# Where the range flag of a fused attention and GELU kernel is combined over partitions, and when the engines load it into registers

## The chip, the cores and the metric

The kernel runs on one core of one Trainium2 chip. The metric is the device time of one launch in microseconds (us), the median of several runs of the same kernel on the same inputs.

## The reference

`q`, `k` and `v` have the shape 8 x 8 x 576 x 64 (batch, head, position, head dimension), float32. Attention runs inside chunks of 64 positions, so every batch and head has nine independent chunks. The attention output, laid out as 4608 tokens of width 512, goes through one feed-forward block with exact GELU.

```python
scores = scale * np.matmul(q_c, k_c.transpose(0, 1, 2, 4, 3))
scores = scores - np.max(scores, axis=-1, keepdims=True)
attn = np.exp(scores)
attn = attn / (np.sum(attn, axis=-1, keepdims=True) + 1e-09)
out = np.matmul(attn, v_c)
...
h = x @ w_in                          # 4608 x 512 by 512 x 2048
g = 0.5 * h * (1.0 + erf(h * inv_sqrt2))
return (g @ w_out).astype(np.float32) # 4608 x 2048 by 2048 x 512
```

## The kernel before

The tokens are worked through in nine tiles of 512 (`NT = B + 1 = 9`): one for the first eight chunks of each batch, and a last one for the ninth chunk of all eight batches. A tile goes through three stages: attention of its chunks, the first product with GELU (`mm1_seven`, helper `seven_rows`), the second product (`mm2_seven`). Both products are done block-wise with seven products instead of eight, so VectorE (DVE in the profile) forms sums of blocks between the matmuls, and ScalarE (ACT) applies exp and GELU and copies out of PSUM. TensorE (PE) is kept busy through nearly the whole kernel; the order of the instructions is written out by hand, in tables of steps per tile, so each engine's queue is fixed.

The fast path leaves out the subtraction of the maximum before the exp. That is sound only as long as no softmax sum gets too small or too large. All reciprocals of the sums are therefore kept in three "homes" of 128 partitions (`early`, `ident_f`, and a part of `rest`), and at the end the kernel asks whether all of them lie between 2^-40 and 2^40. If not, `general()` computes everything again, slowly and safely, in a branch that all five engines take together (`tc.If`, at the end of the program). For the inputs measured here the branch isn't taken.

The question is answered in two steps.

- `range_test` runs on VectorE at slot 6 of the last tile's second product (`e2.setdefault(6, ...)`). Three reductions take the minimum of each home and three the maximum, two comparisons and one more minimum make `good`, one number per partition that is 1 where all is in range.
- `range_count`, after the last tile, multiplies `good` by a column of ones on TensorE, which adds it over the 128 partitions; VectorE copies the count from PSUM to SBUF as an integer (`total`). Then `nc.values_load(total)` loads it into a register of each of the five engines, and the branch compares it with 128.

A register load appears in the trace as TENSOR_LOAD, one for each engine. Five engines means five queues: PE's, DVE's, ACT's, GpSimd's (POOL) and SyncE's (SP). SP issues nearly all stores to DRAM; ScalarE issues some of the last ones.

The last tile's second product ends like this, and here the order around the change is set. Its seven products use three PSUM banks, of which "a" is split in two halves (`m = 0, 1`) of 256 columns. What comes out of them is combined and stored in this order: `done(0, 0)` early (line 726, stores at line 874), then `done(0, 1)` and `done(1, 1)` (line 726 again: one operation on 512 columns, then two on 256), each with its stores at line 874, then `last_piece` twice (line 978: VectorE copies half a bank to `y_sb`; line 981: SP and ScalarE store one half each). TensorE can start the last product on a half of bank "a" only after VectorE has read that half at line 726. After the branch come twelve semaphore waits on SP for all stores and queues, and a barrier of the five engines (all under line 1363, which is the end of the program).

Of the kernel before, what the change touches and what calls it, by code (L numbers as in the profile page):

```python
# [11 lines left out]
def kernel(  # L12
# [9 lines left out]
    nc = tc.nc  # L22
    P = 128
    f32 = mybir.dt.float32
    bf16 = mybir.dt.bfloat16
# [7 lines left out]
    G = H // 2  # L33
# [27 lines left out]
    QD = P // G  # L61
# [17 lines left out]
    NB = MT // 32  # L79
    late = rest[:].bitcast(f32)[:, 256 - 14 * NB:256]  # L80
    homes = [None, ident_f[:], late]
# [26 lines left out]
    work = ctx.enter_context(tc.tile_pool(name="work", bufs=3))  # L108
# [5 lines left out]
    ps_at = ctx.enter_context(tc.tile_pool(name="ps_at", bufs=3, space=bass.MemoryType.PSUM))  # L114
# [452 lines left out]
    def sums_home():  # L567

        raw = stage_tile()[:].rearrange("p (g i n) -> p g i n", g=2, i=4)
        w_in_sum.append([raw[:, 0, i].bitcast(bf16).rearrange("p (k n) -> p k n", k=2) for i in range(4)])  # L570
        kept_more.extend(raw[:, 1, 2 * i:2 * i + 2] for i in range(2))
# [302 lines left out]
            by.dma_start(rows.rearrange("m p d -> p m d"), y_sb[i * CH:(i + 1) * CH])  # L874

    LOW, HIGH = 2.0 ** -40, 2.0 ** 40
    verdict = []

    def range_test():

        assert used == [h.shape[-1] for h in homes]
        n = len(homes)
        for a, op in enumerate((mybir.AluOpType.min, mybir.AluOpType.max)):
            for i, home in enumerate(homes):
                nc.vector.tensor_reduce(ends[:, a, i:i + 1], home, axis=mybir.AxisListType.X, op=op)
        nc.vector.tensor_scalar(ok[:, 0:n], ends[:, 0], LOW, None, op0=mybir.AluOpType.is_gt)
        nc.vector.tensor_scalar(ok[:, n:2 * n], ends[:, 1], HIGH, None, op0=mybir.AluOpType.is_lt)
        nc.vector.tensor_reduce(good, ok, axis=mybir.AxisListType.X, op=mybir.AluOpType.min)
        verdict.append(good)

    def range_count():

        count = ps_at.tile([1, 1], f32, tag="at", name="count")
        nc.tensor.matmul(count[:], ones_1, verdict[0], start=True, stop=True)
        nc.vector.tensor_copy(total, count[:])

    def general():

# [130 lines left out]
    def phase(t, extra2, by_rows=False, first=0, extra1={}, seven=False):  # L1029
        nms = MT // P  # L1030
        order = [(ms, qt) for ms in range(nms) for qt in range(NQ)]
        if by_rows:
            order = [(None, f) for f in range(FF - FC)] + [(ms, NQ - 1) for ms in range(nms)]
        if t not in DENSE:
            mm1_seven(t, extra1)
        else:
            for f in range(first, FF):
                for u in extra1.get(f, ()):
                    u()
                mm1_slot(t, f)  # L1040
        if seven:
            mm2_seven(t, extra2)
            return
        for s, (ms, qt) in enumerate(order):
            for u in extra2.get(s, ()):
                u()
            if ms is None:
                mm2_rows(t, qt)
            else:
                mm2_slot(t, ms, qt)  # L1050
        for u in extra2.get("end", ()):
            u()
# [33 lines left out]
    act_scratch = consts.tile([P, 1], f32, name="act_scratch")  # L1086
    small = consts.tile([P, 28], f32, name="small")
    ends = small[:, 0:6].rearrange("p (a i) -> p a i", a=2)
    ok, good, ones_1 = (small[:, 6:11].bitcast(bf16)[:, a:b] for a, b in ((0, 6), (6, 7), (7, 8)))
    total = small[0:1, 11:12].bitcast(mybir.dt.int32)  # L1090
    nc.gpsimd.memset(ones_1, 1.0)
    homes[0] = consts.tile([P, 3 * NB + 16 + 2 * NB], f32, name="early")[:]

    def act_table(func):
# [2 lines left out]
    with tc.manual_schedule():  # L1097
# [104 lines left out]
        mm, at = (ps_mm, "mm"), (ps_at, "at")  # L1202
# [44 lines left out]
        def flip_qk(t):  # L1247
            for nm in "qk":
                flip(t, nm)
# [6 lines left out]
        for t in range(1, NT):  # L1256
            n = t + 1
            if n < NT:
                tiles[n]["x"] = xpool.tile([P, G, MT], bf16, tag="x", name="x")
            if t == 2:  # L1260
                sums_home()
            if t in STEPS:
                play(t, STEPS[t])
                continue
            if t == 1:
                mm1_slices(1, {0: mm, 1: at, 2: at, 3: mm, 8: mm},
                           (((0, 1, 2), (0,)), last_av, ((0, 1, 2), (1,)), ((3,), (0, 1)), ((8,), (0, 1)),
                            ((0, 1, 2, 3, 8), (2,)), ((0, 3, 8, 1, 2), (3,))))
                x_sums(1)
                for g in range(G):  # L1270
                    cast_qk(2, "k", g, DV)
                flip(2, "q")
                load_v_rows(2, (0,))
                flip(2, "k")
                for ms, y_sb in held:
                    store(0, ms, y_sb)
                held.clear()
                load_v_rows(2, (1,))
                cast_v_rows(2, PO)
                bring_qk(3)  # L1280
            if t > T0 and n + 1 < NT:
                flip_qk(n + 1)
            def next_loads():
                if t + 3 == NT - 1:
                    bring_qk(t + 3)
                elif t + 3 < NT:
                    bring_qk(t + 3)
                if n + 1 < NT:
                    load_v_rows(n + 1)
                    cast_v_rows(n + 1, PO)  # L1290
            if t == T0:
                flip(n + 1, "q")
            elif t > T0:
                next_loads()
            e1, e2 = {}, {}
            exp, gelu = lambda: act_table(Act.Exp), lambda: act_table(Act.Gelu)
            xs = [lambda m=m: quad_x(n, m // 2, m % 2) for m in range(G)]
            g = [[lambda i=i, a=a: g_sum(t, i, a) for i in (1, 2, 4)] for a in range(2)]
            parts = [[lambda m=m: quad_part(t + 2, m // 2, m % 2) for m in ms] for ms in ((1, 0), (3, 2))]
            e1 = {"s3": [lambda: g_sum(t, 3)], "g0": g[0]} if t not in DENSE else {9: [lambda: g_sum(t, 3)], 13: g[0]}  # L1300
            e2 = {0: g[1][:2], 2: g[1][2:]}
            if t <= T0:
                ov = [lambda m=m: quad_over(n, m) for m in range(G)]
                rx = [[lambda m=m: att_rc(n, m), lambda m=m: quad_x_plain(n, m)] for m in range(G)]
                e2 = {0: [exp, lambda: quad_scores(n, ALONE)] + g[1][:2], 2: g[1][2:],
                      4: [lambda: [quad_sums(n), quad_turned(n)]], 5: [ov[0]], 6: [ov[1]],
                      7: [ov[2]] + rx[0], 8: [ov[3]] + rx[1], 9: rx[2], 10: rx[3]}
                e2[{1: 7, 2: 5, T0: 6}[t]].insert(1, lambda: quad_av(n, ALONE))
                if t > 1:
                    e1["x"] = [lambda: x_sums(t)]  # L1310
                if t == T0:
                    e1["g0"] = g[0][:1] + [lambda: w_in_sums(3, (0, 1))] + g[0][1:] + [lambda: w_in_sums(3, (2, 3))]
                if t == 1:
                    e1["w"] = [lambda: weight_sum(2), lambda: weight_sum(3)]
                    e1["w0"] = [lambda: w_in_sums(0, (0, 1))]
                    e1["w1"] = [lambda: w_in_sums(0, (2, 3))]
                    e2[2].append(lambda: weight_sum(4))
                    e2[4].append(lambda: load_qk(4, "q"))
                    e2[7].append(lambda: pool_cast_qk(4, "q"))
                    e2[12] = [lambda: flip_qk(3), lambda: load_qk(4, "k"), lambda: pool_cast_qk(4, "k"),  # L1320
                              lambda: load_v_rows(3), lambda: cast_v_rows(3, PO)]
                else:
                    e1["k"] = [lambda: flip_qk(n + 1) if t < T0 else flip(n + 1, "k"), next_loads]
                if t < T0:
                    e2[11] = [gelu]
                else:
                    e2[2] += [lambda: g_sum(t, 3)]
                    e2[10] += [lambda: quad_scores(n + 1, BETWEEN), gelu]
                    e2[12] = [lambda: x_sums(n)] + parts[0]
                    e2[13] = parts[1]  # L1330
            if t in WHOLE:
                e1, e2 = whole_hooks(t)
            if t == NT - 1:
                e2.setdefault(6, []).append(range_test)
            phase(t, e2, first=5 if t == 1 else 0, extra1=e1, seven=True)
        range_count()
        in_range = nc.values_load(total)
        with tc.If(in_range < P, preferred_fallthrough_block=False):
            general()
# [1 line left out]
_INS = ['q', 'k', 'v', 'moe_w_in', 'moe_w_out']  # L1341
# [26 lines left out]
```

## Time and profile before

| | us |
|---|---|
| median of 3 runs | 266.9 |
| lowest and highest of them | 266.48, 267.42 |
| the profiled execution's own time | 267.09 |
| span of the profiled execution | 265.5 |
| PE busy in the span | 256.1 (96%) |
| DVE busy | 223.1 (84%) |
| ACT busy | 190.5 (72%) |
| POOL busy | 103.2 (39%) |

The span runs from the first to the last instruction in the profile; 267.09 - 265.5 = 1.6 us of the profiled execution lie outside it. Instructions of the sequencers (branches, semaphore waits, register loads, the issuing of DMAs) aren't counted as busy; in the trace their engine's name carries a q (SPq, ACTq).

### The profile page before, as it was taken

What the parts mean: (1) busy time and instruction counts of PE and PEld (TensorE: products, weight loads), DVE (VectorE), ACT (ScalarE), POOL (GpSimd) and SP (SyncE); (2) the same over time, 40 slices, a digit from 0 to 9 for tenths busy, and PEclk for the clock granted to TensorE, in tenths of its full rate; (3) what the DMA queues carried; (4) which work ended last, traced back from release to release, by engine and by line L of the source; (5) the groups of instructions that cost most, each with busy time, mean ns of one, the idle gap of its engine ahead of it and who ended that gap; (6) DMA issues with size and microseconds to landing.
All of it is one profiled execution on the core that took longest, in us unless ns stands there. A gap on an engine that the chain in (4) does not pass through costs nothing.

```text
span 265.5 us, 7854 instructions
## 1 busy us (share of the span) xinstructions
PE 256.1 (96%) x3122; PEld 210.6 (79%) x3122; DVE 223.1 (84%) x394; ACT 190.5 (72%) x386; POOL 103.2 (39%) x225
## 2 busy tenths in 40 slices
PE   6789999999999999999999999999999999999993
PEld 2478875556888888887888888888888888888882
DVE  6874986898897599678999999999999999948772
ACT  3856758987767987898888588947894789227720
POOL 7767778702364291481372095009411300000000
PEclk9999999999999999999999999999999999999998
DMA  6999998999979979999999988998973410130014
GB/s 201 268 311 396 395 401 236 283 193 289 243 195 284 220 175 244 275 239 249 276 245 232 267 186 237 217 175 195 264 160 80 134 42 2 41 119 3 2 40 125
DMA packets 123416, 54.02 MB, mean 203 GB/s; under 512 B 97776, under 2 KB 120304, under 8 KB 123376
## 3 DMA queue, kind: packets, MB, share of 16 engines
q1 hardware_dynamic: 123072, 53.23, 77.4%
q8 instruction: 25, 0.41, 0.7%
q10 hardware_dynamic: 304, 0.26, 0.3%
q14 instruction: 15, 0.12, 0.1%
HBM read 36.70 MB, written 9.44 MB: 174 GB/s over the span
## 4 chain that ended last, share of the span: by engine, by line
PE 76%; DMA 10%; ACT 7%; SPq 4%; issue 1%; DVE 0%; POOL 0%
PE hs_ps L601 31%; PE y_ps L761 22%; PE y_ps L791 13%; DMA arrival<-in_moe_w_out_dram 8%; ACT h L609 3%; SPq L181 2%; PE h_ps L491 2%; DMA arrival<-in_moe_w_in_dram 2%; PE av_ps L349 2%; PE h_ps L481 2%; ACT pT L272 2%; SPq L142 1%; PE y_ps L1025 1%; PE y_ps L989 1%; PE s_ps L264 1%; ACT L1095 1%
## 5 line engine op out<-in xcount | busy, mean ns | idle before, releaser
L609 ACT ACTIVATE h<-hs_ps 128x512 bf16<-128x512 f32 x87 | 49.6, 609 | 6.5 <-PE hs_ps L601 5.7
L238 POOL CAST v_nat<-arrival 128x256 bf16<-128x256 f32 x56 | 24.9, 473 | 33.5 <-DMA arrival<-in_v_dram 23.1
L601 PEld LDWEIGHTS <-w_in_sb 128*128 128x128 bf16 x348 | 33.9, 98 | 4.7 <-issue 0.2
L194 POOL CAST q_nat<-arrival 128x256 bf16<-128x256 f32 x40 | 16.8, 467 | 50.2 <-DMA arrival<-in_k_dram 25.3
L601 PE MATMUL hs_ps<-x,w_in_sb 128*128 128x256 bf16 x232 | 31.8, 272 | 0.0
L761 PEld LDWEIGHTS <-h 128*128 128x128 bf16 x240 | 23.2, 98 | 2.8
L1095 ACT ACT_TABLE_LOAD x16 | 20.5, 1283 | 1.3 <-PEq L1352 1.0
L190 POOL CAST k_nat<-arrival 128x256 bf16<-128x256 f32 (+1 forms) x44 | 19.1, 476 | 5.3 <-DMA arrival<-in_k_dram 5.3
L721 ACT COPY kept<-y_ps 128x512 f32<-128x512 f32 (+1 forms) x17 | 9.0, 536 | 16.0 <-PE y_ps L761 15.9
L761 PE MATMUL y_ps<-w_out_sb,h 128*128 128x256 bf16 x160 | 18.6, 273 | 0.0
L761 PE MATMUL y_ps<-v_bd,k_bd 128*128 128x256 bf16 x160 | 18.5, 273 | 0.1
L761 PEld LDWEIGHTS <-k_bd 128*128 128x128 bf16 x160 | 15.6, 98 | 2.1 <-issue 0.2
L618 ACT COPY hs_ps<-hs_ps 128x512 f32<-128x512 f32 x29 | 16.2, 583 | 0.6 <-PE hs_ps L601 0.5
L601 PE MATMUL hs_ps<-k_bd,w_in_sb 128*128 128x256 bf16 x116 | 16.6, 272 | 0.0
L493 ACT ACTIVATE h<-h_ps 128x512 bf16<-128x512 f32 x21 | 12.5, 604 | 5.5 <-PE h_ps L465 4.1
L272 ACT ACTIVATE pT<-s_ps 128x512 bf16<-128x512 f32 x28 | 14.4, 599 | 1.8 <-PE s_ps L264 1.8
L791 PEld LDWEIGHTS <-h 128*128 128x128 bf16 x144 | 13.8, 98 | 1.7
L465 PE MATMUL h_ps<-x,w_in_sb 128*128 128x256 bf16 x128 | 14.5, 273 | 0.1
L601 PE MATMUL hs_ps<-k_bd,w_in_more 128*128 128x256 bf16 x96 | 14.2, 273 | 0.0
L601 PEld LDWEIGHTS <-w_in_more 128*128 128x128 bf16 x128 | 12.5, 98 | 2.0 <-issue 0.3
L726 DVE TENSOR_TENSOR kept<-y_ps,kept 128x512 f32<-128x512 f32 (+1 forms) x16 | 10.4, 651 | 4.3 <-PE y_ps L761 2.3
L465 PEld LDWEIGHTS <-w_in_sb 128*128 128x128 bf16 x128 | 12.3, 98 | 2.1 <-DVE w_in_sb L1070 0.7
(175 smaller groups left out, 638.9 us busy)
## 6 DMA issues: line engine op xcount, KB each, us to landing
arrival<-in_v_dram SPq DMA_DIRECT2D x58, 128.0 KB, 3.2
arrival<-in_k_dram SPq DMA_DIRECT2D x28, 256.0 KB, 5.6
arrival<-in_q_dram SPq DMA_DIRECT2D x7, 1024.0 KB, 6.9
out_dram<-kept SPq DMA_DIRECT2D x24, 256.0 KB, 3.2
arrival<-in_moe_w_out_dram SPq DMA_DIRECT2D x4, 1024.0 KB, 12.1
arrival<-in_moe_w_in_dram SPq DMA_DIRECT2D x6, 512.0 KB, 8.5
out_dram<-y_sb SPq DMA_DIRECT2D x8, 256.0 KB, 2.5
arrival<-in_v_dram SPq DMA_DIRECT2D x28, 64.0 KB, 2.7
```

What stands on the lines that cost most here:

```text
L190: copy(st[nm][:, q0:q0 + n, g], st[nm + "f"][:, 2 * q0:2 * (q0 + n), g].rearrange("p (q r) d -> p q r d", r=2))
L194: copy(st[nm][:, g, j:j + 2].rearrange("p j r d -> p r j d"), st[nm + "f"][:, 2 * g:2 * g + 2, j:j + 2])
L238: copy(st["v"][:, r::2, n], st["vf"][:, r::2, n])
L272: nc.scalar.activation(pT[:].rearrange("p u (c j) -> p u c j", j=J), tiles[t]["s_ps"][m // 2][m % 2][:].rearrange("p u (j c) -> p u c j", ...
L465: nc.tensor.matmul(to[:, cols], left, right[:, cols], start=(start and a == 0), stop=stop, skip_group_check=True)
L493: nc.scalar.activation(tiles[t]["h"][:, f, :], h_ps[:], Act.Gelu)
L601: nc.tensor.matmul(hs[:, f], left[:, ks, f * P:(f + 1) * P], right[:, ks], start=(fresh and f == 0 and ks == 0), stop=(ks == 1), skip_grou ...
L609: nc.scalar.activation(h[:, n:n + HM, HD * c:HD * (c + 1)], src, Act.Gelu)
L618: "s11": lambda: AC(place_of("b")[:], bank["a"][:]),
L761: nc.tensor.matmul(to, left(f, m), right[:, f], start=(fresh and (split or m == 0) and f == 0), stop=(f == HF - 1), skip_group_check=True)
L791: nc.tensor.matmul(bank[name][:, m], left(f, m), right[:, f], start=(fresh and m == 0 and f == 0), stop=(f == HF - 1), skip_group_check=True)
L1095: nc.scalar.activation(act_scratch[:], rest[:, 0:1], func)
```

## The change

The combination over partitions moves from TensorE to VectorE and into `range_test`, right behind `good`. A 32 x 32 block transpose of `good`, spread over 32 columns, puts the 32 numbers of each of the four partition groups into rows; a reduction takes the minimum of each row; three operations on single numbers take the minimum of the groups at partitions 0, 32, 64 and 96; a comparison turns it into `bad`, an integer that is 1 when anything was out of range. The matmul, its copy, and GpSimd's memset of the column of ones go. `ok` and `good` are float32 instead of bfloat16.

The five register loads are split. SP and GpSimd load `bad` at the end of `range_test`, that is at slot 6 of the last tile; ScalarE at slot 10 of it; TensorE and VectorE where all five stood before, after the last tile. The branch tests the register itself.

```diff
     LOW, HIGH = 2.0 ** -40, 2.0 ** 40
-    verdict = []
...
-        n = len(homes)
+        MIN, n = mybir.AluOpType.min, len(homes)
...
-        nc.vector.tensor_reduce(good, ok, axis=mybir.AxisListType.X, op=mybir.AluOpType.min)
-        verdict.append(good)
-
-    def range_count():
-
-        count = ps_at.tile([1, 1], f32, tag="at", name="count")
-        nc.tensor.matmul(count[:], ones_1, verdict[0], start=True, stop=True)
-        nc.vector.tensor_copy(total, count[:])
+        nc.vector.tensor_reduce(good, ok, axis=mybir.AxisListType.X, op=MIN)
+        turned = work.tile([P, NB, 32], f32, tag="rc", name="turned", bufs=4)[:, 0]
+        nc.vector.transpose(turned, good.to_broadcast([P, 32]))
+        nc.vector.tensor_reduce(good, turned, axis=mybir.AxisListType.X, op=MIN)
+        for s in range(1, G):
+            nc.vector.tensor_tensor(good[0:1], good[0:1], good[QD * s:QD * s + 1], op=MIN)
+        nc.vector.tensor_scalar(bad, good[0:1], 0.5, None, op0=mybir.AluOpType.is_lt)
+        read_flag((mybir.EngineType.SP, mybir.EngineType.Pool))
+
+    flag = nc.alloc_registers("flag")
+
+    def read_flag(engines):
+        for reg in flag:
+            if reg.engine in engines:
+                nc.reg_load(reg, bad)
...
-    ok, good, ones_1 = (small[:, 6:11].bitcast(bf16)[:, a:b] for a, b in ((0, 6), (6, 7), (7, 8)))
-    total = small[0:1, 11:12].bitcast(mybir.dt.int32)
-    nc.gpsimd.memset(ones_1, 1.0)
+    ok, good = small[:, 6:12], small[:, 12:13]
+    bad = small[0:1, 13:14].bitcast(mybir.dt.int32)
...
             if t == NT - 1:
                 e2.setdefault(6, []).append(range_test)
+                e2.setdefault(10, []).append(lambda: read_flag((mybir.EngineType.Activation,)))
             phase(t, e2, first=5 if t == 1 else 0, extra1=e1, seven=True)
-        range_count()
-        in_range = nc.values_load(total)
-        with tc.If(in_range < P, preferred_fallthrough_block=False):
+        read_flag((mybir.EngineType.PE, mybir.EngineType.DVE))
+        with tc.If(flag, preferred_fallthrough_block=False):
             general()
```

Three queues change near the end. SP's, before: the stores of whole blocks (line 867), five stores of line 874, two of line 981, then the register load and the branch.

```order
L867 DMA out_dram<-kept 128x2x256 x3
L867 DMA out_dram<-y_sb 128x2x256
L874 DMA out_dram<-kept 64x2x256 x5
L981 DMA out_dram<-y_sb 64x256 x2
L1337 TENSOR_LOAD small
L1338 COMPARE_AND_BRANCH
L1338 UNCONDITIONAL_BRANCH
```

And SP's queue after the change, from the same place on (the later lines have moved by five or six numbers):

```order
L867 DMA out_dram<-kept 128x2x256 x3
L867 DMA out_dram<-y_sb 128x2x256
L874 DMA out_dram<-kept 64x2x256 x2
L901 TENSOR_LOAD small
L874 DMA out_dram<-kept 64x2x256 x3
L987 DMA out_dram<-y_sb 64x256 x2
L1343 COMPARE_AND_BRANCH
L1343 UNCONDITIONAL_BRANCH
```

The load has moved ahead of the last five stores of SP, and nothing but the branch stands behind them now. On ScalarE it moves in the same way, ahead of its three stores, and on GpSimd it stays last.

VectorE's queue before, from the last step of `range_test` to the branch:

```order
L888 TENSOR_REDUCE small<-small 128x1
L726 TENSOR_TENSOR kept<-y_ps,kept 128x512
L726 TENSOR_TENSOR kept<-y_ps,kept 128x256 x2
L978 COPY y_sb<-y_ps 128x256 x2
L895 COPY small<-count 1x1
L1337 TENSOR_LOAD small
L1338 COMPARE_AND_BRANCH
```

The same stretch of VectorE's queue after the change (line 887 is the former 888, line 984 the former 978):

```order
L887 TENSOR_REDUCE small<-small 128x1
L889 STREAM_TRANSPOSE turned<-small 128x32
L890 TENSOR_REDUCE small<-turned 128x1
L892 TENSOR_TENSOR small<-small 1x1 x3
L893 TENSOR_SCALAR small<-small 1x1
L726 TENSOR_TENSOR kept<-y_ps,kept 128x512
L726 TENSOR_TENSOR kept<-y_ps,kept 128x256 x2
L984 COPY y_sb<-y_ps 128x256 x2
L901 TENSOR_LOAD small
L1343 COMPARE_AND_BRANCH
```

Six operations have come in ahead of line 726, and the copy of the count behind line 978 has gone. Everything earlier in the program stands in the same order on every engine, apart from GpSimd's one memset at the start.

## The prediction

> **What bounds the kernel now.** I began with the page: its span, the busy times and the chain that ended last.
>
> ```profile
> span 265.5 us, 7854 instructions
> PE 256.1 (96%) x3122; PEld 210.6 (79%) x3122; DVE 223.1 (84%) x394; ACT 190.5 (72%) x386; POOL 103.2 (39%) x225
> PE 76%; DMA 10%; ACT 7%; SPq 4%; issue 1%; DVE 0%; POOL 0%
> ```
>
> TensorE bounds the body, and the change touches nothing in it. So I turned to the end of the chain, in order of time (start, length, what):
>
> ```profile
> 255.00 6.24 PE y_ps L761 x57
> 261.26 0.42 DVE y_sb L978
> 261.68 0.05 DVE small L895
> ```
>
> The last matmul that matters ends at 261.2, VectorE's last half block at 261.68, the count 0.05 later. The span ends at 265.5. Nearly 3.8 us belong to no busy engine, and they must be read from the queues. Here are the five register loads and what SP does behind its own (durations in ns, first and last start in us), and the last stores with the time from issue to landing:
>
> ```profile
> L1337 POOLq TENSOR_LOAD <-small x1: 587/587/587, 261.8 to 261.8; - x1
> L1337 DVEq TENSOR_LOAD <-small x1: 607/607/607, 261.8 to 261.8; - x1
> L1337 PEldq TENSOR_LOAD <-small x1: 596/596/596, 261.8 to 261.8; - x1
> L1337 SPq TENSOR_LOAD <-small x1: 952/952/952, 262.2 to 262.2; - x1
> L1337 ACTq TENSOR_LOAD <-small x1: 920/920/920, 262.3 to 262.3; - x1
> L1338 SPq COMPARE_BRANCH  x2: 38/50/61, 263.3 to 263.4; - x2
> L1363 SPq EVENT_SEMAPHORE  x12: 28/28/28, 263.9 to 264.6; - x12
> 261.71 0.49 SPq L981 DMA_DIRECT2D out_dram<-y_sb  x1
> out_dram<-y_sb SPq DMA_DIRECT2D x1, 64.0 KB, 1.9
> out_dram<-y_sb ACTq DMA_DIRECT2D x1, 64.0 KB, 2.2
> ```
>
> SP issues its last store at 261.71 for 0.49 us, then loads the flag from 262.25 to 263.20, branches, and walks through twelve waits from 263.9 to 264.6. About 0.9 us of barrier follow to 265.5. The stores land at 261.71 + 1.9 = 263.6 (SP) and 261.71 + 2.2 = 263.9 (ScalarE). The twelve waits follow each other evenly, (264.6 - 263.9) / 11 = 0.06 us apart, so none of them is held: the data is there before SP asks. That the transfers are over can be seen in the windows (the last two numbers are DMA share and GB/s):
>
> ```profile
> 263.30:263.60 0.30, 0.00 (x0) 0.00 (x0) 0.00 (x0) 0.00 (x0) 0.00 (x0) 1.00 0.52 127
> 263.60:263.80 0.20, 0.00 (x0) 0.00 (x0) 0.00 (x0) 0.00 (x0) 0.00 (x0) 0.74 0.00 0
> ```
>
> The end is therefore bound by SP's queue: last store, load, branch, waits. The landing of the stores comes second, closely behind.
>
> **What the change takes off the end.** On SP nothing but the branch stands behind the last store. Its issue ends at 261.71 + 0.49 = 262.20, the branch comes where the load stood, and all that follows on SP is 0.95 + 0.05 = 1.0 us earlier: the first of the twelve waits at 262.9 instead of 263.9. ScalarE gains about as much and isn't last. TensorE and VectorE still load at the end, but without waiting for the count: from about 261.3 and 261.7 at the latest, 0.6 us, so they are through by 262.3 and have 1.5 us before SP's barrier.
>
> Now the landings are late. SP's last store lands at 261.71 + 1.95 = 263.66, and the wait for it holds SP there. How many waits remain behind it decides the gain. No view prints which wait is for which store; in the operands that the trace keeps, the fifth of the twelve names the semaphore of SP's last store and the twelfth that of ScalarE's. So SP stands at the fifth until 263.66, needs seven more steps of 0.06, that is 0.45 with the restart, and passes the twelfth at 264.1, where ScalarE's store has been since 263.9. Before, the twelfth wait began at 264.6. The gain is 264.6 - 264.1 = **0.5 us** (0.47 from the unrounded starts). Its bounds: had the latest landing to be waited for first, 263.9 + 0.7 = 264.6, no gain; had it to be waited for last, 264.6 - 263.95 = 0.65. With no landing in the way it would be 1.0.
>
> **What the change adds to VectorE.** The six new operations lie behind `good`; these rows show the stretch, with the idle time in brackets:
>
> ```profile
> 256.33 0.17 DVE L887 TENSOR_SCALAR small<-small 128x3 bf16<-128x3 f32 x1
> 256.54 0.16 DVE L888 TENSOR_REDUCE small<-small 128x1 bf16<-128x6 bf16 x1
> 257.82 0.69 DVE L726 TENSOR_TENSOR kept<-y_ps,kept 128x512 f32<-128x512 f32 x1 [1.12 <-PE y_ps L761]
> 258.64 0.42 DVE L726 TENSOR_TENSOR kept<-y_ps,kept 128x256 f32<-128x256 f32 x1
> 259.31 1.91 PE L761 MATMUL y_ps<-v_bd,h 128*128 128x256 bf16 x16
> ```
>
> VectorE idles for 1.12 us from 256.70 to 257.82, waiting for TensorE. That is the cover. For prices I take VectorE's nearest forms (busy us, mean ns of one):
>
> ```profile
> L309 DVE STREAM_TRANSPOSE rc<-rest 128x512 f32<-128x512 f32 x12 | 8.4, 701 | 0.1
> L287 DVE STREAM_TRANSPOSE pt<-pT 128x256 f32<-128x256 f32 x16 | 6.9, 434 | 0.0
> L885 DVE TENSOR_REDUCE small<-early 128x1 f32<-128x96 f32 x2 | 0.5, 246 | 0.0
> L885 DVE TENSOR_REDUCE small<-rest 128x1 f32<-128x224 f32 x2 | 0.7, 374 | 0.0
> L299 DVE TENSOR_TENSOR total<-part 32x64 f32<-32x64 f32 x16 | 3.5, 217 | 0.3
> L886 DVE TENSOR_SCALAR small<-small 128x3 bf16<-128x3 f32 x1 | 0.2, 159 | 0.0
> L895 DVE CAST small<-count 1x1 int32<-1x1 f32 x1 | 0.1, 134 | 0.0
> ```
>
> Transpose: (701 - 434) / 256 = 1.04 ns an element, so 32 elements cost 434 - 224 x 1.04 = 200 ns. Reduction: (374 - 246) / 128 = 1.0, so 246 - 64 = 182 ns. The three operations on single numbers: 217 - 63 = 154 ns each from line 299; the cast of one number bounds them below at 134, line 299 itself above at 217. The comparison: 159 as at line 886. Each waits for the one before; from the end of line 887 (256.33 + 0.17) to the start of 888 are 0.04 us, six times 0.24. Sum: 0.20 + 0.18 + 0.46 + 0.16 + 0.24 = **1.24 us**, with bounds of 1.2 and 1.5. `bad` is ready at 256.70 + 1.24 = 257.94.
>
> That is 0.12 beyond the cover: line 726 starts at about 257.98 instead of 257.82 and ends at 258.67, so the next one, on half a block, starts at 258.68 instead of 258.64 and ends at 259.10. TensorE needs that half at 259.31. So 0.2 us of slack are left, and TensorE and both operations of line 978 stay where they were. I cost this at nothing; the cover is gone when `bad` comes later than 258.15, and from there each us costs a us.
>
> **What the early loads hold up.** SP's load waits for `bad`, and its three stores of line 874 are queued behind it; on ScalarE there is a hole, on GpSimd no later work:
>
> ```profile
> 258.54 2.02 SPq L874 DMA_DIRECT2D out_dram<-kept  x3
> 256.01 0.37 ACT L721 COPY kept<-y_ps 128x256 f32<-128x256 f32 x1 [0.50 <-PE y_ps L761]
> 260.02 0.74 ACTq L874 DMA_DIRECT2D out_dram<-kept  x1
> POOL 7767778702364291481372095009411300000000
> ```
>
> Before, the first store went out at 258.54; with line 726 0.16 late it is ready at 258.70. SP's load starts at 257.95. At 0.59 us it ends at 258.54 and holds nothing. At 0.95 it ends at 258.90 and holds the first store until 258.95, 0.4 late in all. I take 0.59: the loads that ran at 0.92 and 0.95 both followed directly on the issue of a store, which this one doesn't. Even at 0.95 the delay melts away. The three issues fill 2.02 us and hold a wait of about 0.15; the last of them would end at 260.9 instead of 260.56, line 981 starts its first store at 260.83 and its second at 261.71, and only the first would move, by 0.1. ScalarE loads somewhere between 258 and 259 in a hole that reaches from 256.4 to 260.0. GpSimd's digits are zero there. At the start of the kernel GpSimd loses one short memset of about 0.1 us off the chain, worth nothing.
>
> The Trainium skill, "DMA: Bandwidth & Descriptors", section "Latency and other measured facts", gives a `tensor_load` a floor of about 600 ns. The loads of GpSimd, VectorE and TensorE agree with 587 to 607, those of SP and ScalarE don't with 952 and 920. By the page's figure the load taken off SP would be worth 0.65 instead of 1.0, and the sum the same, since the landing decides either way.
>
> **The sum.** Off the end 0.47, on VectorE, SP and ScalarE nothing: 267.09 - 0.47 = 266.62 for the profiled execution. That lay 0.19 above the median of the runs, so 266.9 - 0.47 = **266.4 us**, 0.18% less. A measurement of this kernel can tell about 0.3%, or 0.8 us, from no change; the three runs shown lie 0.94 apart. So the likeliest outcome is a real gain that is too small to be told.
>
> **The rivals.**
>
> *The whole 1.0 us comes back.* The landing would have to come earlier too, by 0.5: 266.9 - 1.0 = 265.9. For it: with the loads spread out, the last stores could be written faster. Against it: their issue hangs on line 978 at 261.68, which doesn't move, and once issued they no longer depend on the queue of SP or ScalarE. Chance 0.12.
>
> *Nothing comes back.* The stores ahead of the last one move by up to 0.4 and push the last landing, or the waits are met in another order: 0 to 0.2 of gain, 266.8. For it: the DMA share is 0.52 to the very end, so a late store can collide. Chance 0.13.
>
> *Slower, by a stall at the branch.* In the trace SP takes 0.5 us from its second branch (263.4) to the first wait (263.9). If the code behind the branch had to be fetched from DRAM and only the 0.95 us of the load hid it, the branch would come 1.0 earlier and then wait as long as a small transfer takes, 1.9 by the store's row: 262.4 + 1.9 = 264.3 for the first wait, 0.4 later than now, and 267.3. It decides once that gap exceeds 1.5. Against it stand the queues that moved anything from 263.0 to 263.8:
>
> ```profile
> q10 hardware_dynamic: 80, 0.07, 31.7%
> q1 hardware_dynamic: 52, 0.04, 18.2%
> ```
>
> Both carry stores; a queue of instructions (the page names them so) isn't among them. The Trainium skill, "Runtime: NRT & Kernel Launch", section "Instruction fetch mechanics", has the rule behind this rival, that a taken branch out of the fetched window stalls for a fetch; the trace before shows no such fetch at this branch. Chance 0.05.
>
> *Slower, by VectorE.* If the four operations on single numbers took twice their price, 0.4 each with their gaps, and transpose and reduction their 0.46 with gaps, that would be 2.06, `bad` would come at 258.76, TensorE would wait 258.76 - 258.15 = 0.6, and against the gain 0.14 would be lost: 267.0. It decides from 258.6 on, and tells by the measure only from 259.4. Chance 0.05.
>
> **How the numbers follow.** The forecast keeps 0.65. Faster by over 0.3% (under 266.1) is nearly all of the first rival, 0.11, and a fifth of the forecast, since medians of a few runs stray by some tenths: 0.24. Slower by over 0.3% (over 267.7) would take the worse halves of the two last rivals and some straying: 0.06. The rest, 0.70, is within. The range reaches from the first rival's 265.9 to 267.0, which holds the second and leaves out the slower ones and strayed runs.
>
> **What would show it.** In the profile after: SP's first exit wait near 262.9; a gap inside the twelve waits that ends near 263.7; the twelfth near 264.1 and the span near 265.1; SP's load near 257.95; line 726 at about 257.98; TensorE's last product still at 259.31. Wrong would be an even row of waits that ends before 263.8 (the landing doesn't hold SP), a last product later than 259.4 (VectorE's cover was too short), or stores of line 981 issued later than 261.75.

## The result, and the profile after

| | median us | lowest to highest |
|---|---|---|
| before | 266.81 (14 runs) | 265.98 to 267.81 |
| after | 268.68 (14 runs) | 267.54 to 270.58 |

The ratio is 1.0068, with a 95% interval from 1.005 to 1.0086: 1.8 us slower, where 0.5 us faster had been forecast. Among all runs of this document one counts as slow, 269.26 us of the kernel called "no code to jump over" below; its ratio leaves that run out (median 266.03 with it, 265.99 without). The profiled execution after took 270.58 us, the longest of the fourteen, with a span of 268.9 us. Its last half block is copied 1.9 us later than in the profile before; this moment differs as much between profiles of kernels whose body is the same (see below the table of the runs). So all tails here are counted from the end of that copy, the second line 978 before and 984 after.

First the part that the change was about. Here are VectorE's operations from `good` on, then the three early loads and the two late ones:

```profile
258.44 0.16 DVE L887 TENSOR_REDUCE small<-small 128x1 f32<-128x6 f32 x1
258.64 0.21 DVE L889 STREAM_TRANSPOSE turned<-small 128x32 f32<-128x32 f32 x1
258.88 0.18 DVE L890 TENSOR_REDUCE small<-turned 128x1 f32<-128x32 f32 x1
259.10 0.52 DVE L892 TENSOR_TENSOR small<-small 1x1 f32<-1x1 f32 x3
259.65 0.14 DVE L893 TENSOR_SCALAR small<-small 1x1 int32<-1x1 f32 x1
259.76 1.21 DVE L726 TENSOR_TENSOR kept<-y_ps,kept 128x512 f32<-128x512 f32 x2
263.16 0.42 DVE L984 COPY y_sb<-y_ps 128x256 f32<-128x256 f32 x1 [0.45 <-PE y_ps L761]
```

```profile
L901 SPq TENSOR_LOAD <-small x1: 470/470/470, 259.8 to 259.8; - x1
L901 ACTq TENSOR_LOAD <-small x1: 472/472/472, 259.8 to 259.8; - x1
L901 POOLq TENSOR_LOAD <-small x1: 490/490/490, 259.8 to 259.8; - x1
L901 PEldq TENSOR_LOAD <-small x1: 513/513/513, 261.9 to 261.9; - x1
L901 DVEq TENSOR_LOAD <-small x1: 606/606/606, 263.2 to 263.2; - x1
```

From the end of line 887 (258.60) to the end of 893 (259.79) are 1.19 us. From the start of the first line 726 to the end of the last copy are 263.58 - 259.76 = 3.82 us, before 261.68 - 257.82 = 3.86: nothing behind the six operations is late. TensorE runs its last products in one piece, without a gap (start, length, from the chain that ended last):

```profile
254.94 8.20 PE y_ps L761 x75
```

SP's early load takes 0.47 us, from 259.82 to 260.29, and the next store is issued only at 260.48, so it holds no store:

```profile
260.48 1.99 SPq L874 DMA_DIRECT2D out_dram<-kept  x3
```

Now SP's waits at the end, and the two last stores with the time to landing (SP, ScalarE):

```profile
L1368 SPq EVENT_SEMAPHORE  x4: 28/28/28, 264.8 to 265.0; - x4
L1368 SPq EVENT_SEMAPHORE  x8: 28/28/28, 267.6 to 268.0; - x8
```

```profile
out_dram<-y_sb SPq DMA_DIRECT2D x1, 64.0 KB, 3.9
out_dram<-y_sb ACTq DMA_DIRECT2D x1, 64.0 KB, 4.1
```

The first wait stands 1.2 us behind the copy, before it was 2.2: that is the 1.0 us off SP's exit. But behind the first four waits SP is held for 2.5 us at the fifth, the one for its last store, since that store lands 3.9 us after its issue instead of 1.9. These windows show why: the queues that moved anything from 264.7 to 265.5, then the windows from 265.5 on, in which the last two numbers are the share of the sixteen DMA engines and GB/s:

```profile
q10 hardware_dynamic: 84, 0.07, 31.6%
q1 hardware_dynamic: 75, 0.06, 29.9%
q8 instruction: 1, 0.02, 8.7%
```

```profile
265.50:266.30 0.80, 0.00 (x0) 0.00 (x0) 0.00 (x0) 0.00 (x0) 0.00 (x0) 0.86 0.05 20
266.30:267.30 1.00, 0.00 (x0) 0.00 (x0) 0.00 (x0) 0.00 (x0) 0.00 (x0) 0.50 0.06 11
```

The stores (q1 and q10) are nearly through by 265.5. Among them stands one packet of 16 KB from q8, a queue of instructions; 8.7% of sixteen engines over 0.8 us is 1.1 us on one engine. From 265.5 to 266.3 no store moves at all, and then the rest follows alone. This is what the DMA view counts from 266.3 to 267.3:

```profile
DMA packets 14, 0.01 MB, mean 11 GB/s; under 512 B 3, under 2 KB 14, under 8 KB 14
```

Fourteen packets at a share of 0.06, that is one engine in sixteen. In the trace's semaphore events 15 of the 16 parts of SP's last store had landed by 265.55; the sixteenth came at 267.55. ScalarE's last two stores each have one late part too, at 267.40 and 267.70, where their other fifteen had landed by 265.19 and 265.84. The trace doesn't name the DMA engine of a packet; that these parts and the q8 packet share one is read from this. The packet's 1.1 us isn't the whole delay of 2.0: the part that came at 267.40 was overdue already when the packet started (265.26), and why isn't shown. Before the change the same q8 packet comes too, but it has the time after 263.6 to itself, with the stores done (the windows of the prediction show a share of 0.00 there). The queues of the kernel before from 263.6 to 264.9:

```profile
q14 instruction: 3, 0.02, 5.9%
q8 instruction: 1, 0.02, 4.9%
```

Who sends for it? TensorE's branches, before and after (first and last start):

```profile
L1338 PEldq COMPARE_BRANCH  x2: 91/198/304, 262.5 to 262.8; - x2
```

```profile
L1343 PEldq COMPARE_BRANCH  x2: 90/200/310, 262.5 to 263.3; - x2
L1368 PEldq DRAIN  x1: 312/312/312, 263.7 to 263.7; - x1
```

Before, TensorE's second branch came 1.1 us behind the end of the last copy, since its load waited for the count; after, it comes 0.3 us ahead of it, as soon as TensorE has done its last matmul. The last stores are issued at that very time. That q8 is TensorE's queue was a guess at this point; the experiments had to bear it out.

### The profile page after: what moved, and what is told of

Read it like the earlier page. It is cut to its first block, busy times and chain, and to the rows that moved or that the text cites. A ratio compares the mean times of both kernels' runs of the same rounds, so it can differ in the third digit from the quotient of the medians.

```text
span 268.9 us, 7850 instructions
## 1 busy us (share of the span) xinstructions
PE 258.0 (96%) x3115; PEld 211.7 (79%) x3121; DVE 225.1 (84%) x399; ACT 190.6 (71%) x386; POOL 104.7 (39%) x224
## 4 chain that ended last, share of the span: by engine, by line
PE 68%; SPq 11%; DMA 10%; ACT 5%; issue 1%; POOL 1%; DVE 1%; POOLq 0%
PE hs_ps L601 26%; PE y_ps L761 18%; PE y_ps L791 9%; DMA arrival<-in_q_dram 6%; DMA arrival<-in_moe_w_in_dram 4%; SPq L136 4%; SPq L152 4%; PE h_ps L465 3%; ACT h L609 3%; PE y_ps L1031 3%; SPq L181 2%; PE h_ps L481 2%; PE h_ps L491 2%; PE av_ps L349 1%; PE y_ps L995 1%
## 5 line engine op out<-in xcount | busy, mean ns | idle before, releaser
L190 POOL CAST k_nat<-arrival 128x256 bf16<-128x256 f32 (+1 forms) x44 | 20.1, 500 | 5.1 <-DMA arrival<-in_k_dram 5.0
L605 DVE TENSOR_TENSOR hs_ps<-hs_ps,kept_p 128x512 f32<-128x512 f32 x15 | 10.3, 690 | 3.5 <-PE hs_ps L601 3.1
```

The source lines that it names most:

```text
L190: copy(st[nm][:, q0:q0 + n, g], st[nm + "f"][:, 2 * q0:2 * (q0 + n), g].rearrange("p (q r) d -> p q r d", r=2))
```

## The experiments

The **fetch theory**: TensorE's early branch sets off the transfer of a block of code, which stands in front of the last stores on one DMA engine. Its rivals: the **early-load theory** (loads ahead of the stores do the harm) and the **VectorE theory** (the six operations do). All kernels are edits of the changed kernel. Five of them use a copy of the flag that VectorE makes behind its last half block, so that who loads the copy must wait for it (`read_flag` gets what to load as a second argument, which isn't shown):

```diff
+    late = small[0:1, 14:15].bitcast(mybir.dt.int32)
...
+        nc.vector.tensor_copy(late, bad)
-        read_flag((mybir.EngineType.PE, mybir.EngineType.DVE))
+        read_flag((mybir.EngineType.PE, mybir.EngineType.DVE), late)
```

All results together, from twelve runs each (nine for "only TensorE early"). The tail is the time from the end of VectorE's last half block copy to the end of the span. The next two columns are the starts of TensorE's second branch and of q8's last packet, counted from the end of that copy. These three are from the unrounded times of the profiled execution.

| kernel | median us | ratio to before, 95% interval | tail us | branch us | q8's packet us | landing of SP's last store us |
|---|---|---|---|---|---|---|
| before | 266.8 to 266.9 | | 3.86 | +1.1 | +2.2 | 1.9 |
| after | 268.68 | 1.0068 (1.005 to 1.0086) | 5.35 | -0.3 | +1.7 | 3.9 |
| TensorE and VectorE late | 266.1 | 0.9965 (0.9948 to 0.9982) | 3.37 | +1.1 | +2.6 | 2.0 |
| TensorE late | 266.16 | 0.9972 (0.9948 to 0.9995) | 3.37 | +1.4 | +2.4 | 2.0 |
| VectorE late | 268.13 | 1.0043 (1.0022 to 1.0064) | 5.12 | -0.3 | +1.1 | 3.7 |
| only TensorE early | 268.09 | 1.006 (1.0036 to 1.0085) | 5.07 | -0.3 | +1.1 | 3.7 |
| no code to jump over | 266.03 | 0.9969 (0.9944 to 0.9994) | 3.35 | -0.9 | none | 2.0 |
| four matmuls more | 266.01 | 0.9974 (0.995 to 0.9999) | 3.37 | +0.6 | +1.9 | 2.0 |
| eight matmuls more | 266.93 | 0.9985 (0.9956 to 1.0014) | 3.36 | +1.5 | +2.5 | 2.0 |
| all five late | 266.74 | 0.9987 (0.9962 to 1.0012) | 3.88 | +1.0 | +2.0 | 2.0 |

The copy ends anywhere from 260.6 to 263.6 in these ten profiles, though the edits leave the work ahead of it almost untouched; that is the spread of the body, and the runs carry it too. The tails fall into three groups, and inside each they agree within 0.3 us, in two of them within 0.03. The medians lie somewhat further apart than the tails (changed kernel against the one with TensorE and VectorE late: 2.6 against 2.0). That difference lies within the intervals, and no run explains it.

The two columns in the middle say whose packet it is and when it does harm. It starts 1.0 to 1.9 us behind TensorE's second branch in all nine kernels that have it. In the kernels in which nothing holds them, the last store packets end 1.9 us behind the copy (1.89 to 1.91 in the trace). Where q8's packet starts at +1.9 or later the store lands in 1.9 to 2.0 us; where it starts at +1.7 or earlier the store lands in 3.7 to 3.9.

**TensorE and VectorE late.** The edit is the one above.

> TensorE and VectorE load the flag from a copy that VectorE makes behind its last half block, so both branch about where they did in the kernel before; SP, ScalarE and GpSimd stay early as in the changed kernel, and the six operations stay. Fetch theory (TensorE's early branch sends for 16 KB of code that stand in front of the last stores on one DMA engine): the last store lands about 2 us after its issue again, no hole in SP's twelve waits beyond 0.6 us, time 266.3 to 266.6 against 266.8 before, that is 0.1 to 0.2% faster. Early-load theory (the loads ahead of the stores do the harm): stays at 268.7. VectorE theory (the six operations delay TensorE): stays at 268.7.

SP's load, TensorE's branches and SP's twelve waits, by line:

```profile
L901 SPq TENSOR_LOAD <-small x1: 472/472/472, 257.4 to 257.4; - x1
L1345 PEldq COMPARE_BRANCH  x2: 90/197/304, 261.9 to 262.2; - x2
L1370 SPq EVENT_SEMAPHORE  x12: 28/28/28, 262.3 to 263.6; - x12
```

266.1 us, 0.35% faster than before. TensorE's second branch stands at 262.2, the copy ends at 261.13. In this profile the twelve waits reach from 262.3 to 263.6, 1.3 us: more than the 0.7 of an even row, so SP is still held at the landing, but only until it has taken its 2.0 us. The twelfth wait begins 2.43 us behind the copy, before it was 2.92. That is the forecast's 0.5 us. The median is below the 266.3 to 266.6 that I had expected: the runs put the gain at 0.9 us (0.5 to 1.4), and what makes it more than the tail shows isn't known. The early loads of SP, ScalarE and GpSimd and the six operations are in this kernel, so neither rival theory holds.

**One of the two.** In the first of this pair only TensorE's load is behind the copy, in the second only VectorE's:

```diff
-        read_flag((mybir.EngineType.PE, mybir.EngineType.DVE))
+        read_flag((mybir.EngineType.DVE,))
+        nc.vector.tensor_copy(late, bad)
+        read_flag((mybir.EngineType.PE,), late)
```

```diff
-        read_flag((mybir.EngineType.PE, mybir.EngineType.DVE))
+        read_flag((mybir.EngineType.PE,))
+        nc.vector.tensor_copy(late, bad)
+        read_flag((mybir.EngineType.DVE,), late)
```

> As the first, but only TensorE's load is behind the copy; VectorE loads ahead of it. Fetch theory with TensorE as the fetcher: like the first, 266.3 to 266.8. If VectorE's early branch did the harm: 268.7. Early-load theory and VectorE theory: 268.7.

> Only VectorE's load is behind the copy; TensorE loads as early as in the changed kernel. Fetch theory with TensorE as the fetcher: as the changed kernel, 268 to 269.5, the last store's landing 3 us or more after its issue. If VectorE's early branch did the harm: 266.3 to 266.8.

266.16 and 268.13 us: the harm follows TensorE's load and not VectorE's. (The first is just below the 266.3 to 266.8 that I had expected.) The second profile shows the picture of the changed kernel again, first by line, then VectorE's last copy in order of time, then ScalarE's last store in the DMA view:

```profile
L1346 PEldq COMPARE_BRANCH  x2: 90/200/310, 261.2 to 262.0; - x2
L1371 SPq EVENT_SEMAPHORE  x12: 27/28/28, 263.5 to 266.5; - x12
```

```profile
261.87 0.42 DVE L984 COPY y_sb<-y_ps 128x256 f32<-128x256 f32 x1 [0.45 <-PE y_ps L761]
```

```profile
out_dram<-y_sb ACTq DMA_DIRECT2D x1, 64.0 KB, 3.9
```

TensorE branches before the copy ends at 262.3, SP's waits reach over 3.0 us, and ScalarE's last store takes 3.9 us to land.

**Only TensorE early.** SP's, GpSimd's and ScalarE's early loads are taken away, and they and VectorE load the copy at the end:

```diff
-        read_flag((mybir.EngineType.PE, mybir.EngineType.DVE))
+        read_flag((mybir.EngineType.PE,))
+        nc.vector.tensor_copy(late, bad)
+        read_flag((mybir.EngineType.DVE, mybir.EngineType.SP, mybir.EngineType.Pool, mybir.EngineType.Activation), late)
```

> SP, ScalarE, GpSimd and VectorE load at the end from the copy, as in the kernel before; only TensorE loads early. Fetch theory: slow too, 268 to 269, since SP now asks at about the same place as before but the last store lands 2 us late. Early-load theory: back to 266.8, since no load stands ahead of a store.

TensorE's branches and SP's last store:

```profile
L1344 PEldq COMPARE_BRANCH  x2: 90/200/310, 259.6 to 260.4; - x2
out_dram<-y_sb SPq DMA_DIRECT2D x1, 64.0 KB, 3.7
```

268.09 us, with no load of SP or ScalarE ahead of their stores. This settles the early-load theory: TensorE's early load alone is enough. It also parts q8 from q14, the other queue of instructions: q8's packet starts at 261.71, when the stores are under way, the first of the three from q14 only at 262.78, when 15 of the 16 parts of SP's last store have landed (by 262.61).

**No code to jump over.** The loop with the recomputation is taken out of the branch's body, so that what is left behind the branch is only the loading of the weights, which has no matmul. The loads of the flag stay where the changed kernel has them. The other engines' code behind the branch gets shorter too, and TensorE's second branch no longer stands behind a semaphore wait.

```diff
-        with tc.For_i(0, B, 1) as b:
-            with tc.For_i(0, S, CH) as s0:
-                one_chunk(b, s0, SUBS)
```

> The changed kernel, loads where it has them, but the branch's body keeps only the loads of the weights: the recomputation by chunks is left out, so TensorE has almost no code to jump over. Fetch theory (16 KB of TensorE's code are sent for because the jump leaves the fetched block): no 16 KB packet after the last branch, last store lands 2 us after its issue, time 266.0 to 266.5. If it is not the fetch but the early branch itself (TensorE's early drain, or its early wait): 268.0 to 268.8 as with the jump.

The page's row of q8 and, for comparison, the one of the changed kernel below it; then TensorE's branches and SP's last store of this kernel:

```profile
q8 instruction: 24, 0.39, 0.6%
```

```profile
q8 instruction: 25, 0.41, 0.6%
```

```profile
L1340 PEldq COMPARE_BRANCH  x2: 85/132/180, 259.8 to 259.9; - x2
```

```profile
out_dram<-y_sb SPq DMA_DIRECT2D x1, 64.0 KB, 2.0
```

266.03 us. TensorE branches even earlier here, at 259.9 and so 0.9 us ahead of the copy's end, but q8 has 24 packets instead of 25, with none at the end, and SP's last store lands in 2.0 us. So it isn't the early branch that hurts but the packet that it sets off. This kernel alone wouldn't say whose queue q8 is, since q14 has 12 packets here instead of 15; the pair above does, in which q8's packet moved with TensorE's load (+2.4 and +1.1 us in the table).

**TensorE kept busy.** TensorE gets matmuls on 512 columns behind its last product, four in one kernel and eight in the other; all loads stay as in the changed kernel.

```diff
+        idle = ps_at.tile([P, MT], f32, tag="at", name="idle")
+        for _ in range(4):
+            nc.tensor.matmul(idle[:], w_in_sb[:, 0, 0:P], w_in_sb[:, 0, 0:MT], start=True, stop=True)
         read_flag((mybir.EngineType.PE, mybir.EngineType.DVE))
```

> The changed kernel with four matmuls on 512 columns behind TensorE's last product, whose result nobody reads: TensorE's second branch comes 0.9 us later, about 0.6 us after VectorE's last half block is copied (changed kernel: 0.3 us before it; kernel before: 1.1 us after it). Fetch theory: a branch's packet starts 1.0 to 1.4 us after the branch, so about 1.6 to 2.0 us behind the copy, at the tail of the last stores' packets: in between, 266.3 to 267.8, with a larger spread of the runs. If only the loads' places matter: 268.4, and TensorE's additional work would be hidden.

> The same with eight matmuls: the branch comes 1.7 us later than in the changed kernel, 1.4 us after the copy. Fetch theory: the packet starts behind the last store's packets, time 266.0 to 266.5 although TensorE does more. If only the loads' places matter: 268.4 or more.

TensorE's branches and SP's twelve waits in the kernel with four:

```profile
L1346 PEldq COMPARE_BRANCH  x2: 90/197/304, 259.9 to 261.6; - x2
L1371 SPq EVENT_SEMAPHORE  x12: 28/28/28, 262.1 to 263.4; - x12
```

266.01 us with four: work that TensorE doesn't need makes the kernel 2.7 us faster by the medians than without it, 2.0 by the tails. I had expected 266.3 to 267.8; four are enough, since with the branch at 261.6, 0.6 us behind the copy, q8's packet starts at 262.85, just as the last store packet ends. With eight the runs missed my numbers, 266.93 us instead of at most 266.5, and their interval holds no change; the profiled tail, 3.36 us, is that of the good kernels. Where the rest of that median comes from isn't shown.

**All five late.** This kernel asks what each part of the gain is worth. The three early loads are taken away, and all five engines load the copy:

```diff
-        read_flag((mybir.EngineType.PE, mybir.EngineType.DVE))
+        nc.vector.tensor_copy(late, bad)
+        read_flag((mybir.EngineType.PE, mybir.EngineType.DVE, mybir.EngineType.SP, mybir.EngineType.Pool, mybir.EngineType.Activation), late)
```

> The combination stays on VectorE (six operations more), but all five engines load the flag at the end, from the copy behind the last half block. What it tells apart: if the gain of the first experiment comes from SP's load off its exit, this stands at 266.6 to 267.0, no change against the kernel before, and the six operations cost nothing; if it comes from the matmul and copy that went, 266.1 to 266.3; if the six operations cost something, 267.1 or more.

SP's load and its twelve waits:

```profile
L900 SPq TENSOR_LOAD <-small x1: 965/965/965, 261.9 to 261.9; - x1
L1368 SPq EVENT_SEMAPHORE  x12: 27/28/28, 263.5 to 264.2; - x12
```

266.74 us, no difference to before that the interval shows (1.0 us faster to 0.3 slower); the tail is 3.88 against 3.86. So the six operations that came and the matmul and copy that went make no difference together, within that interval. The tail, counted from a point behind the six operations, can't show their price. The gain lies in the loads that the first experiment has early and this one late. They are SP's, ScalarE's and GpSimd's, and no run moved SP's alone. That it is SP's is read from the profiles: the first of SP's waits stands 2.2 us behind the copy here, 1.2 in the first experiment.

The first experiment beats the kernel before and the changed one: it is the changed kernel with one VectorE operation more.

## Why the prediction was wrong

**The gain** was right in place and, by the profiles, in size. SP's first wait came 1.2 us behind the copy as forecast, SP was held at the fifth wait as forecast, and where the store landed in its 2.0 us, in the first experiment, the twelfth wait began 0.49 us earlier, against 0.47 forecast (the runs there put the gain at 0.5 to 1.4). The whole 1.0 us of the first rival did not come.

**VectorE** was right: 1.19 us against 1.24, and TensorE ran on without a gap. Two sums beside it are a little off, without effect on the forecast: the upper bound of the six operations comes to 1.43 by the prices given, not 1.5, and the last of SP's three delayed issues would end at 258.95 + 2.02 - 0.15 = 260.8, not 260.9. **The stores behind the early loads** were right: 0.47 us instead of the 0.59 that I took, nothing held.

**The step that failed** is in the part on what the change takes off the end: TensorE and VectorE "still load at the end, but without waiting for the count", through by 262.3 and with 1.5 us to spare. I counted that as harmless, because I asked only whether TensorE would be late for the barrier. I didn't ask what else its branch issues. A moved step carries its transfers along, and this one carries 16 KB on one DMA engine. Before, the wait for the count had kept that packet behind the last store, by an accident of 0.2 us: the stores' share of the DMA engines falls to zero at 263.6, and the packet starts at 263.84 in the trace. The price in the profiles is 5.35 - 3.37 = 2.0 us of tail; less the 0.5 gained, 1.5 is left, against 1.8 (1.3 to 2.3) measured in the runs.

**The rival that came near** was the stall at the branch. It had the fetch, on the wrong engine and with the wrong victim: I priced it as time that SP would wait for its own code, and dismissed it by the queues up to 263.8. That "the trace before shows no such fetch at this branch" holds for that window only: the packet starts at 263.84, just behind it. In fact TensorE didn't wait for the packet: its drain ran at 263.7, and the packet started at 265.26. The stall that the Trainium skill describes in "Runtime: NRT & Kernel Launch", section "Instruction fetch mechanics", a taken branch that waits for its target, isn't what cost the time. The stores paid. The range failed with it: its upper end, 267.0, held no case in which the last landing itself gets later by more than tenths.

## What to carry to other kernels

Before you take away a wait, list everything that the waiting engine issues behind it, its instruction fetches too, and see what they will then run beside. At the end of this kernel the landing of the last store was the bound or nearly so, and one late part in sixteen was enough to hold it; look in the DMA view for a last trickle at a share of 0.06. And where a jump over much code near the last stores sets off such a packet, let that engine branch late enough for the stores to get through first.

## What the runs showed of the hardware

- A packet from the queue that follows TensorE's branch, 16 KB, took 1.0 to 1.6 us at the end of these kernels. Where it came among the last stores, one part in sixteen of SP's and of ScalarE's last store came late: SP's landed 3.7 to 3.9 us after its issue instead of 1.9 to 2.0, in all three kernels in which TensorE branched 0.3 us before the last copy ended.
- TensorE's queue runs ahead of its matmuls: its load ran at 261.9 and its first branch at 262.5 while the last product went on to 263.1. Only the second branch waited; in the kernel without code to jump over it didn't, and came 0.1 us behind the first.
- A register load on SP took 0.47 us where nothing had been issued just ahead of it, and 0.94 to 0.97 directly behind the issue of a store; why wasn't tried. The floor of about 600 ns that the Trainium skill gives in "DMA: Bandwidth & Descriptors", section "Latency and other measured facts", is undercut by the 0.47.
- Whether the 16 KB are the target of the jump or the block behind it stays open; that TensorE went on without them speaks for the block behind.
